# Plain v loaded in pieces of six block columns, with a newly searched fixed order, in a kernel of windowed attention and a gated convolution

## The chip, the core and the metric

The kernel runs on one core of a Trainium2 chip. Five engines work side by side, each through its own queue of instructions in program order: PE (matrix multiply; its weight loads are shown as PEld), DVE (vector), ACT (scalar, exponentials and copies), POOL (general purpose) and SP, which in this kernel only issues DMAs. All DMAs of the kernel are issued from SP, and 16 DMA engines carry them out. The metric is the device time of one execution in microseconds. Three executions of the kernel before took 174.15, 173.76 and 173.53 us; the median is 173.76.

## The reference

Eight batches of eight heads, 576 tokens, 64 features per head. Heads 0 to 3 ("plain") look back over the last 32 tokens, heads 4 to 7 ("dilated") over every fourth of the last 128. The attention's output, 512 features per token, then goes through a gated block: a causal convolution of length 5 gives the gate, a projection gives the value, and a second projection gives the result.

```python
scores = scale * np.matmul(q, k.transpose(0, 1, 3, 2))
mask_plain = (rel >= 0) & (rel < window)
mask_dil = (rel >= 0) & (rel < window * dilation) & (rel % dilation == 0)
attn = softmax(where(mask, scores, -1e9))
x = np.matmul(attn, v)                     # heads side by side: 8 x 576 x 512
gate_pre += conv_w[k][None, None, :] * xp[:, k:k + S, :]     # k = 0..4
gate = 1.0 / (1.0 + np.exp(-gate_pre))
return (gate * (x @ w_val) @ w_out).astype(np.float32)
```

## The kernel before

The program is a list of 733 small tasks, each tied to one engine and to named buffers. A task's name says what it is and of which batch (0 to 7):

- loads on SP: `Lqd`, `Lkd`, `Lvd` bring q, k, v of the dilated heads of a batch, `Lqp`, `Lkp`, `Lvp` those of the plain heads, `Lwv` and `Lwo` the two projection weights, `Lc` the convolution's. For batches 0 and 7 the last fifth of a dilated q or k is a load of its own (`Lqr`, `Lkr`). `ST` stores 128 finished tokens.
- `T` transposes q or k on PE, five matmuls for a dilated half and eighteen for a plain tensor (lines 464 and 401). `E` with q or k in its name copies the result out of PSUM on ACT or DVE (lines 312, 314).
- `S` makes scores of one half (six matmuls, line 333), `E` the exponential on ACT (line 340), `M` the mask multiply on DVE (line 347), `A` the product with v (twelve matmuls, line 356), `N` the division by the row sums on DVE (lines 365, 366). `X` transposes the result back on PE (lines 428, 488), `F` copies it into the gated block's input.
- `U` casts dilated v to bf16 on POOL. For batches 0 to 3 plain v is loaded in natural rows of tokens, and the four shift tasks `HA`, `HB`, `HC`, `HD` (2, 3, 3 and 2 small casts on POOL or ACT, table `SHIFTS`) build the windows that straddle the blocks. For batches 4 to 7 the windows overlap already in the load, and no shift is needed.
- for each pair of batches and each block of tokens, `C` is the convolution on PE (twenty matmuls, line 530), `G` the tanh on ACT, `V` the value projection (eight matmuls, line 548), `Y` the gating on DVE (line 558). `O` is the output projection of 128 tokens (four matmuls, line 577), `EO` its copy out of PSUM (ACT line 584, DVE line 586).
- `Wv` and `Wo` cast the projection weights on POOL; no `V` can start before the three `Wv` tasks, no `O` before the two `Wo`.

The order of everything is fixed by hand-written data. `ORDER` is one word per task: its number, a letter for the engine that runs it, and a number of warm-up matmuls (128x128 by 128x512, line 659) that PE does in front of it into the same PSUM buffer; `HOMES` gives each logical tile its buffer, from `COUNTS` (eight for q and k, two for plain v, three two-bank PSUM tiles, two one-bank ones). Each engine works its words off from left to right, and an engine waits at the head of its queue until the data and the buffer are there. Loads have one rule more: a load waits until the fifth-last "big" load before it has landed (`DEPTH = 5`, `t.after`). The semaphores add another: DMAs take eight semaphores in turn, and a DMA waits for the landing of the one eight places before it in SP's queue.

Before the change plain v of a batch was one DMA, `load_vp`: 18 block columns of 128 rows (2304 packets of 256 bytes) for batches 0 to 3, 24 of them (3072 packets) for batches 4 to 7, counted as a big load.

Of the kernel before, what the change touches and what calls it, by code (L numbers as in the profile page):

```python
# [16 lines left out]
0G 15S 16S 1S 13S 33P6 14S 34A 48S 17S 47S 49S 2P 31P1 32A 3V 18G 38P2 57P 51G 21P 59V 22V 53G 58V 52G 39A 40V  # L17
19P 35P 20A 26P2 36A 23P 80S 27A 37V 24A 28V 25V 41P2 54P 56A 4S 55A 42V 29P 30V 70P 81S 6G 45P3 5G 43P 50A
60P 73P 7S 46V 71A 44A 74A 8G 112S 61A 96P 84P 63P 64A 149P 72V 97A 75V 76P 98P 85V 65V 62V 82S 66P 77V 86P
67V 150A 99A 100P 78P 87A 101A 83G 103P 88P 89A 79V 68P 69V 104A 113S 105V 119P 114S 120A 91P 92A 145P 151P  # L20
93V 102V 90V 121A 94P 169S 146A 152V 106P 95V 147P 122P 107V 108P 170S 110P 123V 124A 138P 109A 201S 139A 148V
135P 185P 136A 125P 128P 129A 126A 111V 165P 166A 140V 130V 137V 116G 127V 186V 234S 202S 157P 158A 187P 115G
118G 117G 141P 171S 175P 176A 188V 192P 193A 131P 142V 132V 173P 172G 174A 189P 190A 208P 209V 210A 143P 133P
177P 178A 180P 203S 134V 211P 235S 250P 144V 159P 181A 213A 212A 227P 228A 153P 154A 11S 238P 205G 251V 194V
179V 191V 160V 182V 239A 206A 195P 229V 196V 207A 167P 168V 204G 12G 183P 184V 155P 252P 224P 225A 214P 240P
215A 9S 253V 156V 199P 254P 241V 255A 226V 217P 218A 161P 230P 197P 162A 200A 324S 267S 236S 216V 219V 245P
256V 220P 198A 246A 231V 10G 625P 628P 221V 323S 266S 325S 237G 626A 257P 242P 243A 276P 629A 222P 326G 223A
258A 278A 277V 163P 341P 232P 303P 247V 244V 259V 233V 342V 304A 299P 300A 164V 339P 260P 248P 329P 305P 330A
340V 268S 261V 631P 630S 355S 384S 533S 627S 346P 356S 249V 343P 264P 306V 265V 273P 632A 347A 344A 348V 274V
275A 272A 345V 262P 301P 302V 279P 280A 292P 634P 635V 263A 349P 350V 327P 293A 328A 289P 281V 282P 283A 290A  # L30
# [72 lines left out]
class Plan:  # L103
# [28 lines left out]
    def run(self):  # L132
# [4 lines left out]
        for word in order:  # L137
# [19 lines left out]
def kernel(  # L157
# [19 lines left out]
    QB = 96  # L177
# [49 lines left out]
    def src_ap(t, offset, ap):  # L227
        return bass.AP(tensor=t.tensor, offset=t.offset + offset, ap=ap)
# [480 lines left out]
```

## Time and profile before

| | us |
|---|---|
| median of three executions | 173.76 |
| the profiled execution, its own time | 173.37 |
| its span, first to last instruction | 171.7 |
| PE busy | 153.0 |
| DVE busy | 121.7 |
| ACT busy | 108.4 |
| POOL busy | 44.2 |

The span is what the trace shows; the time of the execution has 1.7 us more around it. Times of instructions are counted from the span's start. "PE busy" counts pipelined matmuls with modelled ends, so that small idle stretches can hide in it. In the views "A:B" is a stretch of the span, "[1.01 <-DMA ...]" the idle time of an engine in front of an instruction and what ended it, and rows marked "SPq" are DMAs as SP issues them: their duration is the time that the issue held SP, not that of the transfer.

### The profile page before, as it was taken

Reading aid. Unit: us, or ns where it says so; the run is one execution under the profiler, and the core shown is the slowest. Engines: PE = TensorE matmul, PEld = TensorE weight load, DVE = VectorE, ACT = ScalarE, POOL = GpSimd, SP = SyncE. Lnnn points to the kernel's source line nnn. Section 1 sums busy time; section 2 is a strip of 40 time slices with the busy share of each in tenths; the row PEclk is TensorE's granted clock in tenths of the full one; section 3 lists DMA queues with packets and bytes.
Section 4 is the critical chain, followed back from the end, with each engine's and each line's share of the span. In section 5 each row is a group of like instructions: output and inputs, shape, how many; then the busy total and the mean of one; then the engine's idle time right before and its main releaser. Section 6 shows DMA issues by size and latency. Waiting matters only on the chain.

```text
span 171.7 us, 5752 instructions
## 1 busy us (share of the span) xinstructions
PE 153.0 (89%) x2441; PEld 102.2 (60%) x2460; DVE 121.7 (71%) x243; ACT 108.4 (63%) x182; POOL 44.2 (26%) x82
## 2 busy tenths in 40 slices
PE   6697967888989979899999799989999999999990
PEld 1355654677557546567766567576656577666640
DVE  6549778989899579779788658899368776664220
ACT  2147976198868744798847693888946675242542
POOL 7023998560659427403000000210110000000000
PEclk9999999999999999999999999999999999999999
DMA  4999999999799999999994948969979060333445
GB/s 137 325 355 290 375 370 210 311 374 319 200 383 364 362 269 281 373 353 222 282 328 139 267 115 286 373 165 390 270 202 303 2 244 4 116 119 138 186 165 199
DMA packets 49123, 43.63 MB, mean 254 GB/s; under 512 B 22981, under 2 KB 39365, under 8 KB 49098
## 3 DMA queue, kind: packets, MB, share of 16 engines
q1 hardware_dynamic: 49098, 43.27, 82.2%
q8 instruction: 19, 0.31, 0.7%
q14 instruction: 6, 0.05, 0.1%
HBM read 33.83 MB, written 9.44 MB: 252 GB/s over the span
## 4 chain that ended last, share of the span: by engine, by line
PE 58%; DMA 12%; DVE 11%; ACT 6%; SPq 5%; issue 3%; POOL 3%; ACTq 0%; DVEq 0%; POOLq 0%
PE pu L577 17%; PE pd L548 14%; PE pd L530 9%; DMA qk<-in_k_dram 5%; PE pd L356 5%; DVE et L347 4%; DMA wt<-in_moe_w_out_dram 4%; SPq L281 4%; PE pd L333 4%; DMA qk<-in_q_dram 3%; PE pu L464 3%; POOL w_out L316 3%; PE pd L401 2%; PE pu L488 2%; ACT et L340 2%
## 5 line engine op out<-in xcount | busy, mean ns | idle before, releaser
L340 ACT ACTIVATE et<-pd 128x576 bf16<-128x576 f32 x64 | 39.3, 657 | 10.4 <-PE pd L333 9.3
L347 DVE TENSOR_TENSOR et<-et,mask 128x576 bf16<-128x576 bf16 x64 | 33.9, 557 | 4.7 <-ACT et L340 4.5
L548 PE MATMUL pd<-xT,w_val 128*128 128x384 bf16 (+1 forms) x208 | 34.9, 313 | 0.7 <-DVE xn L366 0.4
L577 PE MATMUL pu<-w_out,yT 128*128 128x512 bf16 x127 | 33.4, 379 | 1.4 <-issue 0.6
L558 DVE SCALAR_TENSOR_TENSOR yT<-gate,pd 128x768 bf16<-128x768 bf16 (+1 forms) x26 | 23.0, 886 | 12.5 <-PE pd L548 8.5
L366 DVE TENSOR_TENSOR xn<-pd,rec 96x768 bf16<-96x768 f32 x32 | 30.5, 954 | 1.1
L316 POOL CAST vn<-vd 128x1536 bf16<-128x1536 f32 x8 | 12.3, 1540 | 70.3 <-DMA vd<-in_v_dram 70.3
L540 ACT ACTIVATE gate<-pd 128x768 bf16<-128x768 f32 (+1 forms) x26 | 19.9, 769 | 10.9 <-DVE yT L558 5.5
L548 PEld LDWEIGHTS <-w_val 128*128 128x128 bf16 x208 | 19.4, 97 | 11.6 <-issue 1.5
L530 PE MATMUL pd<-xT,conv_diag 64*64 64x384 bf16 (+1 forms) x520 | 23.1, 313 | 1.8 <-DVE xT L314 1.1
L584 ACT ACTIVATE osb<-pu 128x512 f32<-128x512 f32 x27 | 16.2, 601 | 11.0 <-PE pu L577 10.7
L577 PEld LDWEIGHTS <-yT 128*128 128x128 bf16 x144 | 12.6, 97 | 13.3 <-issue 1.1
L333 PE MATMUL pd<-qT,kT 64*128 64x96 bf16 x384 | 16.1, 209 | 3.1 <-ACT qT L312 0.9
L530 PEld LDWEIGHTS <-conv_diag 64*64 64x64 bf16 x520 | 15.1, 106 | 6.2 <-issue 2.5
L316 POOL CAST vw<-vp 32x384 bf16<-32x384 f32 (+2 forms) x31 | 16.8, 541 | 7.5 <-DMA vp<-in_v_dram 6.1
L356 PEld LDWEIGHTS <-et 128*128 128x128 bf16 x384 | 14.7, 97 | 6.5 <-DVE et L347 2.5
L464 PE MATMUL pu<-ident,qk 128*128 128x128 bf16 x160 | 14.8, 230 | 3.0 <-DMA qk<-in_k_dram 2.0
L333 PEld LDWEIGHTS <-kT 64*128 64x128 bf16 x384 | 10.1, 96 | 11.5 <-issue 6.3
L464 PEld LDWEIGHTS <-qk 128*128 128x128 bf16 x160 | 10.8, 102 | 7.3 <-DMA qk<-in_k_dram 3.0
L314 DVE COPY xT<-pu 128x576 bf16<-128x576 bf16 x18 | 10.1, 568 | 4.0 <-PE pu L488 3.1
L312 ACT COPY xT<-pu 128x576 bf16<-128x576 bf16 x14 | 8.9, 646 | 6.2 <-PE pu L428 3.6
L365 DVE RECIPROCAL rec<-pd 96x12 f32<-96x12 f32 x32 | 7.1, 223 | 7.6 <-PE pd L356 4.5
(52 smaller groups left out, 146.2 us busy)
## 6 DMA issues: line engine op xcount, KB each, us to landing
out_dram<-osb SPq DMA_DIRECT2D x36, 256.0 KB, 2.7
vd<-in_v_dram SPq DMA_DIRECT2D x8, 768.0 KB, 9.3
qk<-in_k_dram SPq DMA_DIRECT2D x8, 576.0 KB, 7.8
qk<-in_q_dram SPq DMA_DIRECT2D x8, 576.0 KB, 8.0
qk<-in_q_dram SPq DMA_DIRECT2D x6, 640.0 KB, 9.1
qk<-in_k_dram SPq DMA_DIRECT2D x6, 640.0 KB, 8.7
vp<-in_v_dram SPq DMA_DIRECT2D x4, 768.0 KB, 7.9
vp<-in_v_dram SPq DMA_DIRECT2D x4, 576.0 KB, 9.8
```

What stands on the lines that cost most here:

```text
L316: nc.gpsimd.tensor_copy(out_, in_)
L333: nc.tensor.matmul(out=ps2[ps.idx][:, l, QB * jj:QB * jj + QB], lhsT=kT[kt.idx][rb, c:c + 128], rhs=qT[qt.idx][rb, c:c + QB], start=True, ...
L340: nc.scalar.activation(out=et[e.idx][:, 0:2 * HW].rearrange("p (l n) -> p l n", l=2), in_=ps2[ps.idx][:, :, 0:HW], func=AF.Exp, scale=scale)
L347: (nc.vector if eng == DVE else nc.gpsimd).tensor_tensor(out=ev, in0=ev, in1=m, op=ALU.mult)
L356: nc.tensor.matmul(out=ps2[po.idx][:, hf, (2 * jj + l) * DA:(2 * jj + l + 1) * DA], lhsT=et[es[hf].idx][:, c:c + 128], rhs=val(j, l), star ...
L366: nc.vector.tensor_tensor(out=xn[xt.idx][0:QB].rearrange("p (h j) l d -> p h (j l) d", h=2), in0=a[:, :, :, 0:D], in1=rr[:, :, :, None].to ...
L464: nc.tensor.transpose(out=o[:, f:f + 128], in_=a[:, c * RD + 128 * cb:c * RD + 128 * cb + 128], identity=ident)
L530: nc.tensor.matmul(out=dst(ps2[pc.idx][64 * ob:64 * ob + 64, n, 0:wd]), lhsT=conv_diag[rb, 2 * cp + n, kk, :], rhs=mov(2 * cp + n, rb, c0 ...
L540: nc.scalar.activation(out=gate[gt.idx][:, :, 0:wd], in_=ps2[pc.idx][:, :, 0:wd], func=AF.Tanh, scale=0.5)
L548: nc.tensor.matmul(out=dst(ps2[pv.idx][:, n, 0:wd]), lhsT=w_val[:, mc, c * 128:(c + 1) * 128], rhs=mov(mc, slice(0, 128), c0), start=(mc = ...
L558: nc.vector.scalar_tensor_tensor(out=yT[yb.idx][:, 2 * cp:2 * cp + 2, t0:t0 + wd], in0=gate[gt.idx][:, :, 0:wd], scalar=1.0, in1=ps2[pv.id ...
L577: nc.tensor.matmul(out=ps1[po.idx], lhsT=yT[yb.idx][:, c, c0:c0 + 128], rhs=w_out[:, c, :], start=(c == 0), stop=(c == NCH - 1))
```

## The change

`load_vp` now makes three DMAs (batches 0 to 3) or four (4 to 7), each of six block columns, 768 packets. They don't count as big, so that they wait for a big load but no later load counts them. The four numbers of `SHIFTS` that are durations for the search's model are changed; the program doesn't read them. `ORDER` and `HOMES` are new throughout: 753 words, 20 of them the added loads.

```diff
-0G 15S 16S 1S 13S 33P6 14S 34A 48S 17S 47S 49S 2P 31P1 32A 3V 18G 38P2 57P 51G 21P 59V 22V 53G 58V 52G 39A 40V
...
+0G 15S 1S 16S 33P6 2P 13S 14S 34V 48S 31P1 32A 59P2 51S 38P 35P 36A 39A 47S 50S 17S 21P 3V 18G 19P 20A 61A 22A
...
-            if t.load:
+            if t.load and eng == SP:
                 t.after = big[-DEPTH] if len(big) >= DEPTH else None
...
     def load_vp(b, ten):
         nat = b < NAT
 
-        def issue():
-            if nat:
-                o, a = vp[ten.idx][:, 0:18, 0:D], [[D, 128], [128 * D, 18], [1, D]]
-            else:
-                o, a = vp[ten.idx][:, :, 0:D], [[D, 128], [QB * D, 4 * NB], [1, D]]
-            return nc.sync.dma_start(out=o, in_=src_ap(v, (b * H * S - (0 if nat else W)) * D, a))
-        return [load(f"Lvp{b}", ten, issue)]
+        def issue(c):
+            o = vp[ten.idx][:, c:c + 6, 0:D]
+            step = 128 if nat else QB
+            return nc.sync.dma_start(out=o, in_=src_ap(v, (b * H * S - (0 if nat else W) + c * step) * D,
+                                                       [[D, 128], [step * D, 6], [1, D]]))
+        parts = [lambda c=c: issue(c) for c in range(0, 18 if nat else 4 * NB, 6)]
+        return [load(f"Lvp{b}", ten, part, big=False) for part in parts]
```

The engines' shares of the tasks change too. DVE has 185 tasks where it had 173: it takes three more output copies `EO` (12 for 9), 3 more dilated k copies, 1 plain k, 2 dilated q, 3 plain q; of the copies into the gated block's input it takes 2 more dilated and 2 fewer plain ones. ACT has 166 for 176: it loses those, and gains one `HA` and one `HC` from POOL (24 for 26). PE does the same 265 tasks; the warm-up matmuls in front of them are 23 for 16.

SP's queue, in the stretch from plain k of batch 0 on. Names ending in a number are buffers: `qk2` holds plain k of batch 0, `vd0` and `vp0` dilated and plain v of batch 0. Before:

```order
L270 DMA qk2_70<-in_k_dram 128x2x576
L290 DMA vd0_80<-in_v_dram 128x6x256
L270 DMA qk3_71<-in_q_dram 128x2x576
L302 DMA vp0_76<-in_v_dram 128x18x64
L281 DMA qk4_72<-in_q_dram 128x5x256
L627 DMA wt0_82<-in_moe_w_val_dram 128x2x512
L281 DMA qk5_73<-in_k_dram 128x5x256
L627 DMA wt1_83<-in_moe_w_val_dram 128x2x512
L270 DMA qk6_74<-in_q_dram 128x2x576
L290 DMA vd1_81<-in_v_dram 128x6x256
```

The same stretch after the change, from the same load on:

```order
L271 DMA qk2_70<-in_k_dram 128x2x576
L301 DMA vp0_76<-in_v_dram 128x6x64
L271 DMA qk3_71<-in_q_dram 128x2x576
L301 DMA vp0_76<-in_v_dram 128x6x64
L291 DMA vd0_80<-in_v_dram 128x6x256
L301 DMA vp0_76<-in_v_dram 128x6x64
L282 DMA qk4_72<-in_k_dram 128x5x256
L282 DMA qk5_73<-in_q_dram 128x5x256
L282 DMA qk6_74<-in_k_dram 128x5x256
L271 DMA qk7_75<-in_k_dram 128x2x576
L291 DMA vd1_81<-in_v_dram 128x6x256
L628 DMA wt0_82<-in_moe_w_val_dram 128x2x512
```

Dilated v of batch 0 moves behind plain q and two of the three pieces of plain v. Dilated k and q of batch 1 now come before the value weights, and dilated k of batch 2 (`qk6`) stands between them and plain k of batch 1. Plain q of batch 1 (`qk6` before), fifth behind `vp0`, comes only after this excerpt.

POOL's queue around the casts of the output weights (`w_out`, tasks `Wo`) and of plain v of batch 2 (`vp0` into `vw0`, tasks `H`). Before:

```order
L316 CAST vn0_85<-vd0_80 128x24x64
L316 CAST vw0_78<-vp0_76 32x5x64
L316 CAST vw0_78<-vp0_76 32x6x64 x2
L316 CAST vw0_78<-vp0_76 64x6x64 x2
L316 CAST w_out_129<-wt2_84 128x512
L316 CAST w_out_129<-wt2_84 64x512 x2
L316 CAST w_out_129<-wt0_82 64x512 x4
```

And after:

```order
L317 CAST w_out_129<-wt2_84 128x512
L317 CAST w_out_129<-wt2_84 64x512 x2
L317 CAST vn0_85<-vd0_80 128x24x64
L317 CAST vw0_78<-vp0_76 64x6x64 x2
L317 CAST vw0_78<-vp0_76 32x5x64
L317 CAST vw0_78<-vp0_76 32x6x64 x2
L317 CAST w_out_129<-wt0_82 64x512 x4
```

Three of the seven weight casts move ahead of the casts of batch 2; the other four now follow those of plain v directly.

More of the change, by code (lines that the diff above doesn't have):

```diff
@@ L22 @@
[L22 to L30, printed above, removed]
-284V 271G 270G 269G 643P 644A 637P 285P 291V 294V 400P 401V 286V 638A 334P 331P 335A 332A 336V 640P 641A 295P
```

59 lines of the change are left out of this document (35 added, 24 removed), and 6 rows, old and new, of the table SHIFTS.

## Prediction

> **What bounds the kernel now.** I read the page first, then sums by stretch, then PE's idle times, then SP's queue.
>
> ```profile
> PE 153.0 (89%) x2441; PEld 102.2 (60%) x2460; DVE 121.7 (71%) x243; ACT 108.4 (63%) x182; POOL 44.2 (26%) x82
> PE 58%; DMA 12%; DVE 11%; ACT 6%; SPq 5%; issue 3%; POOL 3%; ACTq 0%; DVEq 0%; POOLq 0%
> 0.00:36.00 36.00, 28.00 (x435) 18.07 (x438) 26.61 (x75) 19.54 (x33) 21.41 (x54) 1.00 0.97 301
> 56.30:168.10 111.80, 106.52 (x1654) 70.90 (x1670) 76.82 (x136) 71.73 (x123) 11.76 (x14) 1.00 0.76 229
> ```
>
> The columns of the last two rows are the stretch, its length, PE, PEld, DVE, ACT, POOL busy, granted clock, DMA share, GB/s. Over the whole span PE is the bound, but not everywhere: up to 36 us it is idle for 8 us while the DMAs are busy 97% of the time, and from 56.3 us to its last matmul it is idle for 5.28 us of 111.8. So the first stage is fed by loads, the rest is PE's own work with small holes. The clock is full throughout and is no term here.
>
> ```profile
> 22.46 0.45 PE L464 MATMUL pu<-ident,qk 128*128 128x128 bf16 x5 [1.01 <-DMA qk<-in_k_dram]
> 30.01 0.92 PE L356 MATMUL pd<-vn,et 128*128 128x65 bf16 x24 [1.04 <-DVE et L347]
> 63.50 1.00 PE L530 MATMUL pd<-xT,conv_diag 64*64 64x384 bf16 x18 [1.12 <-DVE xT L314]
> ```
>
> These are PE's longest holes behind a load, a mask and a copy. The change aims at the first kind. Why a load is late there, SP's queue shows:
>
> ```profile
> 4.97 0.78 SPq L302 DMA_DIRECT2D vp<-in_v_dram  x1
> 7.82 5.54 SPq L281 DMA_DIRECT2D qk<-in_q_dram  x1
> 22.43 0.37 SPq L302 DMA_DIRECT2D vp<-in_v_dram  x1
> 23.82 5.13 SPq L281 DMA_DIRECT2D qk<-in_q_dram  x1
> 38.26 5.67 SPq L281 DMA_DIRECT2D qk<-in_k_dram  x1
> ```
>
> In these three cases (the third plain v was issued just ahead of the last row) the DMA behind a plain v holds SP for 5 us, where others take 0.4 to 1: 2304 packets do not fit at once, and SP stands until they have nearly drained. What that costs the DMA engines is in the rows around the second and third such load:
>
> ```profile
> 27.00:28.00 1.00, 0.92 (x16) 0.44 (x8) 0.52 (x3) 1.00 (x3) 1.00 (x4) 1.00 1.31 245
> 28.00:29.00 1.00, 0.97 (x6) 0.39 (x4) 1.00 (x1) 0.71 (x1) 1.00 (x1) 1.00 1.09 193
> 29.00:30.00 1.00, 0.00 (x0) 0.00 (x0) 1.00 (x3) 0.00 (x0) 0.28 (x1) 1.00 0.26 56
> 30.00:31.00 1.00, 0.99 (x25) 0.92 (x26) 0.96 (x3) 0.00 (x0) 0.00 (x0) 1.00 0.66 138
> 31.00:32.00 1.00, 1.00 (x7) 0.58 (x6) 1.00 (x2) 0.00 (x0) 0.40 (x1) 1.00 1.02 339
> 42.00:43.00 1.00, 0.39 (x16) 0.42 (x16) 0.62 (x2) 1.00 (x2) 0.00 (x0) 1.00 1.31 234
> 44.00:45.00 1.00, 1.00 (x11) 0.46 (x10) 1.00 (x3) 0.73 (x2) 0.72 (x1) 1.00 0.25 62
> ```
>
> The small packets run at 245 GB/s, larger ones at 339 and more, but between them there is a hole at 56 and 62 GB/s.
>
> **The change part by part.** I follow two gates, then the rest.
>
> **(a) The holes.** Against the rates beside it the first hole shown loses (245-193)/245 + (245-56)/245 + (339-138)/339 = 0.21 + 0.77 + 0.59 = 1.6 us of transfer. The one at 44 us has the same depth, so 1.6 again. Two holes are 3.2 us by the time the first 24 large loads are in. A piece of 768 packets is as many as a dilated v, whose successors were issued without such a stand. I take the whole 3.2; the bounds are 0 (pieces leave holes too) and 3.2.
>
> **(b) The output weights' gate.** The first output projection needs all seven weight casts.
>
> ```profile
> 50.82 5.49 POOL L316 CAST w_out<-wt 128x512 bf16<-128x512 f32 x7 [1.68 <-DMA wt<-in_moe_w_out_dram]
> 55.89 2.14 PE L577 MATMUL pu<-w_out,yT 128*128 128x512 bf16 x7
> L316 POOL CAST vw<-vp 32x384 bf16<-32x384 f32 x21 | 11.5, 547 | 2.0 <-DMA vp<-in_v_dram 1.0
> L316 POOL CAST w_out<-wt 64x512 bf16<-64x512 f32 x6 | 4.6, 764 | 0.3
> ```
>
> Now the casts end at 50.82 + 5.49 = 56.3 us, just when PE gets there. The last of the 24 loads (through the second half of `w_out`) landed about 52.2: the first half at 50.7, where the casts begin, and 0.52 MB more at 339 GB/s, 1.5 us. After the change the same 24 loads are in front, only the last is the third piece of plain v of batch 2. Without holes it lands at 52.2 - 3.2 = 49.0. POOL then does `HA`, `HB` (5 x 0.547 = 2.7) and four weight casts (4 x 0.764 = 3.1): the gate moves to 54.8. With the holes kept it would be 58.0.
>
> **(c) Does PE get there by then?** PE's own prices come from runs of its tasks without a wait:
>
> ```profile
> 101.16 0.36 PE pd L333 x12
> 101.89 1.30 PE pd L548 x8
> 103.19 0.86 PE pu L577 x4
> 106.66 0.28 PE pu L464 x5
> 106.94 0.94 PE pd L530 x20
> 113.19 0.39 PE pd L356 x12
> 114.18 0.46 PE pu L488 x16
> ```
>
> A plain transpose of q or k takes 0.62, eighteen matmuls at nearly the price of L464's. Up to the transpose of plain k of batch 2 (ending at 43.2 us before) and up to the last dilated score of batch 2 in the new order, both orders have done exactly the same PE tasks, so these two times may be compared. The late load in the new order is plain q of batch 1, now behind dilated k of batch 2. The loads of dilated q of batch 2 and of plain q of batch 1 before, with the time from issue to landing last:
>
> ```profile
> qk<-in_q_dram SPq DMA_DIRECT2D x1, 640.0 KB, 9.5
> qk<-in_q_dram SPq DMA_DIRECT2D x1, 576.0 KB, 9.4
> ```
>
> Issued at 23.82, the first landed at 33.3. The new set up to plain q of batch 1 lacks that load, half of the value weights and two thirds of a plain v, and has one more dilated k of the same size: 0.52 MB (1.5 us at 339 GB/s) and 1536 small packets (1.6 us at 245) less, so 30.2, or 28.6 without the hole at 29 us. I take 29.5. Before, issued at 15.87, it came at 25.3: PE's use of it moves 4 us back, but some 1.5 us of other tasks now stand in front of it. From its transpose (to 30.1) to the common point lie 12.3 us of PE work by the prices above, warm-ups included: 42.4 if nothing waits. Waits I expect: scores of batch 1 behind two ACT copies, 0.5; the first `V` behind the last `Wv` cast, 0.3; the product of batch 1 behind `HC`, `HA` on ACT, 0.5. So **43.7 against 43.2** before, bounds 42.4 and 45.5: no gain in the first stage itself, since the queue brings the same bytes and the new order spends its lead on the wrong load. The seven extra warm-ups are in these sums, 7 x 0.215 = 1.5 us, most in front of tasks that wait for a load anyway; where that cover is gone they cost up to that.
>
> From the common point to the first `O` the new order has 10.8 us: PE arrives at 54.5, and the gate of (b) is at 54.8. Against 56.3 that is **-1.5 us**, bounds -1.5 (the gate holds it even if PE is early) and +1.7 (holes kept). At that point it has one `V` (1.30) more and one `X`, half an `A` and an `S` (0.46 + 0.39 + 0.18) less behind it: **-0.3**.
>
> **(d) The rest, 56 to 168 us.** PE's tasks are the same. No load is near: by the same count of bytes the closest, dilated k of batch 4, lands near 61 and is used near 64. Behind it SP's queue stands at the second store until that output is copied, near 61 too; dilated v of batch 4 and the q loads of 4 and 5 wait behind it, and PE wants them from 72 on. The eight semaphores now cover five large loads and three pieces at a time, some 3.7 MB or 10 us of transfer, so that this wait starves nothing. DVE gets more copies:
>
> ```profile
> L586 DVE TENSOR_SCALAR osb<-pu 128x512 f32<-128x512 f32 x9 | 6.2, 685 | 2.2 <-PE pu L577 2.2
> L314 DVE COPY kT<-pu 128x576 bf16<-128x576 bf16 x6 | 2.7, 446 | 0.0
> L314 DVE COPY kT<-pd 128x576 bf16<-128x576 bf16 x6 | 4.5, 754 | 5.6 <-PE pu L428 3.1 <-PE pd L401 2.2 <-ACT kT L312 0.3
> 30.00:40.00 10.00, 8.98 (x196) 7.03 (x197) 9.29 (x17) 5.90 (x10) 5.38 (x10) 1.00 1.03 345
> 50.00:60.00 10.00, 9.84 (x172) 6.42 (x173) 7.61 (x14) 7.10 (x14) 6.66 (x8) 1.00 1.08 364
> 110.00:120.00 10.00, 9.45 (x211) 6.99 (x211) 9.53 (x18) 8.92 (x17) 1.68 (x1) 1.00 0.89 293
> ```
>
> Three output copies (2.1), five dilated q and k (2.2), four plain (3.0) and the exchanged `F` copies (up to 0.6) are some 7.5 us. A DVE busy 76% left PE 0.16 us idle in ten, one at 93 to 95% left it 0.55 and 1.02. About half the copies fall between 60 and 100 us; if all four stretches of ten there went from the first figure to the last, that would be 4 x 0.86 = 3.4 us. Bounds 0 and 3.4; I take **+0.7**, nearer to nothing because DVE is busy 76.82 of 111.8 us there, 69%. ACT and POOL lose work, and their waits may shrink; I count nothing for it.
>
> **(e) The end.** Before, two output projections stand between the last `V` and the first that needs its gating, now one (0.86 us). `Y` there takes about 0.75 and has two handovers: **+0.15**, bounds 0 and 0.3.
>
> **Sum.** The profiled execution took 173.37, 0.39 less than the median. 173.37 - 1.5 - 0.3 + 0.7 + 0.15 = 172.4; on the median's footing **172.8**.
>
> **The rivals.**
>
> *PE's holes after 56 us close too.* The order was redrawn there as well, and the new one puts more PE work between a task and its user in the first stage. If half of the 5.28 us closes and DVE costs nothing: 172.8 - 2.6 - 0.7 = 169.5. Against it: nothing in the change feeds that stage better, and 95% is already high.
>
> *DVE becomes the late engine.* At the 3.4 us bound, and with the gate's gain kept, 172.8 + 2.7 = 175.5. It decides once DVE passes some 93% over several stretches of ten. For it: DVE holds the longest hole of the rest (1.12, a copy). Against: of the stretches of ten after 60 us only the one at 110 is there now.
>
> *The first stage slips.* Plain q of batch 1 and dilated v of batch 0 come later by 4 and 3 us; if the holes stay and PE reaches the common point at 45.5, the lead is lost and PE gets to the first `O` at 58.0, the gate's other bound: 172.8 + 3.2 = 176.0. Against it: SP's stands of 5 us are plain, and shorter loads behind other loads had none.
>
> *It doesn't do what it says.* The holes close but were hidden: PE reaches the first `O` at 56.3 as before, and what it has done ahead by then (0.3) goes to DVE: 173.8. For it: (c) gives the first stage itself no gain, and PE's way to the gate of (b) has 0.3 us to spare.
>
> *Each DMA has its own price.* Twenty more issues at 0.37 to 1.0 us of SP are 7 to 20 us of an engine that waits most of the time; if a third of the smaller sum came in front of loads that PE needs, 2.5 us: 175.3. Against it, two loads issued one behind the other, 0.5 us apart:
>
> ```profile
> qk<-in_k_dram SPq DMA_DIRECT2D x1, 512.0 KB, 4.2
> qk<-in_k_dram SPq DMA_DIRECT2D x1, 128.0 KB, 4.0
> ```
>
> They land 0.3 us apart, as the smaller one's bytes take. The Trainium skill, DMA: Bandwidth & Descriptors, Rules for kernel authors, speaks against this change: many small transfers should be coalesced into one large one. Its fixed cost of about 2.0 us for each DMA (Anatomy of one DMA, there told of another issuing path) would, paid in a row, make an estimated 40 us for the twenty; by the two rows above it is not paid in a row here.
>
> **How the numbers follow.** A measurement here can tell about 0.3% from no change, 0.5 us. Chances: the forecast 0.38, the holes after 56 us 0.12, DVE 0.20, the slip 0.12, no effect 0.13, SP's price 0.05. The forecast's own range is 171.0 to 174.3, so it holds 0.30 of faster, 0.05 of same, 0.03 of slower. With the others: faster 0.30 + 0.12 + a little of no effect (0.02) = 0.44; same 0.05 + 0.11 = 0.16; slower 0.03 + 0.20 + 0.12 + 0.05 = 0.40. The range 170.0 to 176.0 leaves out half of the second case and the worst of DVE and the slip.
>
> **What would show it.** (a) No issue on SP over 2 us behind plain v before 50 us, and no stretch of 1 us near 60 GB/s. (b) The last weight cast ends near 54.8. (c) PE's last transposes of batch 2 end near 43.7. (d) PE idle from the first `O` to its end 5 to 7 us. Wrong: PE waiting for loads after 60 us, DVE above 93% in several stretches, or the first `O` after 56.3.

## The result and the profile after

Twelve executions of the changed kernel took 173.45 to 174.86 us, median 173.89; twelve of the kernel before 173.22 to 175.22, median 173.86. The ratio is 1.0001, interval 0.9977 to 1.0026: no difference that can be measured, where 172.8 was forecast. (Ratios, here and below, leave out executions that were disturbed, so that one need not be the quotient of two medians.) The profiled execution took 173.49 (before 173.37), its span is 171.7 in both.

The equal times hide two changes of opposite sign. The first two fences are after's page (busy times, chain of waits) and its table by stretches, with the columns of the prediction's.

```profile
PE 154.4 (90%) x2445; PEld 103.0 (60%) x2467; DVE 127.7 (74%) x255; ACT 105.4 (61%) x175; POOL 42.2 (25%) x77
PE 65%; DMA 13%; DVE 10%; SPq 4%; ACT 3%; issue 2%; ACTq 0%; DVEq 0%
```

```profile
28.00:29.00 1.00, 1.00 (x23) 0.65 (x15) 1.00 (x3) 0.59 (x2) 1.00 (x2) 1.00 1.15 288
29.00:30.00 1.00, 0.45 (x11) 0.24 (x7) 1.00 (x4) 1.00 (x2) 1.00 (x3) 1.00 1.10 323
44.00:45.00 1.00, 0.59 (x19) 0.54 (x17) 0.91 (x3) 0.97 (x2) 0.00 (x0) 1.00 1.16 326
58.63:168.30 109.67, 106.56 (x1685) 71.19 (x1700) 82.71 (x147) 67.90 (x114) 10.94 (x12) 1.00 0.70 223
```

DVE is busy 6 us more (127.7), and the chain runs over PE for 65% of the span, not 58, over ACT and POOL for 3, not 9. The holes in the transfer are gone: 323 GB/s at 29 us where before had 56, 326 at 44 us where it had 62. And yet PE's way through the first stage is longer. PE's queue in order of time, at the three places that count:

```profile
30.96 0.69 PE L402 MATMUL pd<-ident,qk 128*64 128x128 bf16 x18 [1.50 <-DMA qk<-in_q_dram]
45.35 0.30 PE L334 MATMUL pd<-qT,kT 64*128 64x96 bf16 x6
58.25 0.24 PE L357 MATMUL pd<-vw,et 128*128 128x65 bf16 x2 [1.26 <-DVE et L348]
58.63 1.02 PE L578 MATMUL pu<-w_out,yT 128*128 128x512 bf16 x3
```

Plain q of batch 1 is waited for until 30.96; the common point, the end of the row at 45.35, is at 45.65 (before 43.24); the first `O` starts at 58.63 (before 55.89). From there to its end PE idles 109.67 - 106.56 = 3.11 us, where it idled 5.28 from 56.30 on before. So 2.7 us are lost up to the first `O` and some 2.5 won behind it.

What holds the first `O`, on POOL and then on DVE:

```profile
50.23 3.24 POOL L317 CAST vw<-vp 64x384 bf16<-64x384 f32 x5 [7.63 <-PE pu L465]
53.53 2.71 POOL L317 CAST w_out<-wt 64x512 bf16<-64x512 f32 x4
56.31 1.58 POOL L317 CAST vn<-vd 128x1536 bf16<-128x1536 f32 x1
```

```profile
55.19 3.00 DVE L348 TENSOR_TENSOR et<-et,mask 128x576 bf16<-128x576 bf16 x3
```

The weights' last cast ends at 56.24, no earlier than before (56.31). The three masks of plain batch 2 run beside POOL's casts and take 3.00 us (the last of them 1.71), where the same three take 1.19 in a run below. SP's longest stand up to 50 us is this one, right behind a piece of plain v; five more issues right behind a piece stand 2.02 to 2.60 us:

```profile
5.89 2.67 SPq L291 DMA_DIRECT2D vd<-in_v_dram  x1
```

### The profile page after: what moved, and what is told of

The parts are those of the page before. It is cut to its first block, busy times and chain, and to the rows that moved or that the text cites. A ratio compares the mean times of both kernels' runs of the same rounds, so it can differ in the third digit from the quotient of the medians.

```text
span 171.7 us, 5799 instructions
## 1 busy us (share of the span) xinstructions
PE 154.4 (90%) x2445; PEld 103.0 (60%) x2467; DVE 127.7 (74%) x255; ACT 105.4 (61%) x175; POOL 42.2 (25%) x77
## 4 chain that ended last, share of the span: by engine, by line
PE 65%; DMA 13%; DVE 10%; SPq 4%; ACT 3%; issue 2%; ACTq 0%; DVEq 0%
PE pu L578 17%; PE pd L549 17%; DMA qk<-in_q_dram 10%; PE pd L531 10%; PE pd L357 5%; PE pd L334 5%; DVE xn L367 3%; PE pu L465 3%; PE pd L402 3%; PE pu L489 2%; DMA qk<-in_k_dram 2%; PE pu L429 2%; DVE et L348 2%; SPq L291 2%; SPq L301 2%
## 5 line engine op out<-in xcount | busy, mean ns | idle before, releaser
L348 DVE TENSOR_TENSOR et<-et,mask 128x576 bf16<-128x576 bf16 x64 | 32.2, 534 | 6.6 <-ACT et L341 6.6
L531 PE MATMUL pd<-xT,conv_diag 64*64 64x384 bf16 (+1 forms) x520 | 23.7, 314 | 0.2
L585 ACT ACTIVATE osb<-pu 128x512 f32<-128x512 f32 x24 | 14.3, 599 | 10.7 <-PE pu L578 10.0
L357 PEld LDWEIGHTS <-et 128*128 128x128 bf16 x384 | 15.3, 97 | 8.0 <-DVE et L348 2.1
L334 PE MATMUL pd<-qT,kT 64*128 64x96 bf16 x384 | 16.7, 207 | 3.3 <-ACT kT L313 0.6
L317 POOL CAST vw<-vp 32x384 bf16<-32x384 f32 (+2 forms) x26 | 16.0, 615 | 12.9 <-PE pu L465 7.6
L531 PEld LDWEIGHTS <-conv_diag 64*64 64x64 bf16 x520 | 14.2, 106 | 4.6 <-issue 0.7
L465 PEld LDWEIGHTS <-qk 128*128 128x128 bf16 x160 | 10.2, 102 | 6.3 <-DMA qk<-in_q_dram 2.4
L402 PE MATMUL pd<-ident,qk 128*64 128x128 bf16 x288 | 11.1, 228 | 2.8 <-DMA qk<-in_q_dram 1.5
L402 PEld LDWEIGHTS <-qk 128*64 128x64 bf16 x288 | 9.4, 115 | 5.3 <-DMA qk<-in_k_dram 1.6
```

Source lines behind the costliest of these rows:

```text
L317: nc.gpsimd.tensor_copy(out_, in_)
L334: nc.tensor.matmul(out=ps2[ps.idx][:, l, QB * jj:QB * jj + QB], lhsT=kT[kt.idx][rb, c:c + 128], rhs=qT[qt.idx][rb, c:c + QB], start=True, ...
L348: (nc.vector if eng == DVE else nc.gpsimd).tensor_tensor(out=ev, in0=ev, in1=m, op=ALU.mult)
L357: nc.tensor.matmul(out=ps2[po.idx][:, hf, (2 * jj + l) * DA:(2 * jj + l + 1) * DA], lhsT=et[es[hf].idx][:, c:c + 128], rhs=val(j, l), star ...
L402: nc.tensor.transpose(out=o[64 * y:64 * y + 64, 128 * j:128 * j + 128], in_=a[:, (y * PJ + j) * D:(y * PJ + j + 1) * D], identity=ident)
L465: nc.tensor.transpose(out=o[:, f:f + 128], in_=a[:, c * RD + 128 * cb:c * RD + 128 * cb + 128], identity=ident)
```

## The experiments

Ratios are to the kernel before, run beside each on the same chip.

### The holes, the pieces and the order, each alone

*Order of before, plain v in pieces, one issued right behind the other:*

```diff
 def load_vp(b, ten):
...
+            for c in range(0, 18 if nat else 4 * NB, 6):
+                got.append(nc.sync.dma_start(
+                    out=vp[ten.idx][:, c:c + 6, 0:D],
...
```

> The order before, with each plain v issued as three or four DMAs of 768 packets one behind the other. If the size of a DMA alone makes the holes in the transfers, they close here too: no stretch of 1 us near 60 GB/s at 29 and 44 us, the loads behind land 1.5 us earlier each time, and by the rigid theory the time falls by up to 1 us, by the absorbed one it stays within 0.5. If it needs other loads between the pieces, SP is still held 4 to 5 us by the third piece or the load behind it, the holes stay, and the time is that of before, 173.8.

Measured: 173.58, ratio 0.9994 (0.9962 to 1.0026). First SP's queue, then the stretches at the second plain v:

```profile
22.39 4.56 SPq L300 DMA_DIRECT2D vp<-in_v_dram  x3
27.06 2.07 SPq L281 DMA_DIRECT2D qk<-in_q_dram  x1
```

```profile
29.00:30.00 1.00, 0.00 (x0) 0.00 (x0) 1.00 (x3) 0.00 (x0) 0.39 (x1) 1.00 1.05 133
30.00:31.00 1.00, 0.88 (x25) 0.85 (x26) 1.00 (x3) 0.00 (x0) 0.00 (x0) 1.00 0.48 121
```

SP stands no shorter than before, only now mostly at the pieces themselves (4.56 + 2.07, before 0.37 + 5.13), and a hole of 133 and 121 GB/s stays. So it is the 2304 small packets in a row that hold SP, not that they were one DMA. Together with the next run, where the new order without pieces holds SP again, this says that other loads between the pieces are what closes the hole.

*Order of after, plain v whole at the place of its last piece:*

```diff
         def issue(c):
+            n = 18 if nat else 4 * NB
+            if c + 6 < n:
+                return None
...
```

> The changed kernel with plain v whole again: one DMA at the place of the last piece, nothing at the others. The holes of 1.5 us come back in the first 60 us. Rigid: PE's first output projection 1 to 3 us later than at 58.6, time 175 to 177. Absorbed: within 0.5 of 173.9. If the pieces were of no use in this order, PE's arrival there does not move either.

Measured: 175.65, ratio 1.0115 (1.0069 to 1.0161). SP's queue, then PE's:

```profile
21.69 6.52 SPq L271 DMA_DIRECT2D qk<-in_q_dram  x1
```

```profile
32.33 0.69 PE L404 MATMUL pd<-ident,qk 128*64 128x128 bf16 x18 [1.77 <-DMA qk<-in_q_dram]
```

SP stands 6.52 us at plain q of batch 1, and PE has it 1.4 us later than in after. In the new order the pieces are worth about 2 us (1.2 to 2.8 by the interval); in the old one (the run above) nothing that can be measured.

### The late load of plain q

*After, with plain q of batch 1 loaded ahead of dilated v of batch 1, and transposed ahead of that batch's first product with v:*

```diff
-... 65P 55A 73A 75P 174S 89A 115S 84S ... 4S 5G 43P 69V 44V 6G 118S 114S 116S ... 96P 123P ...
+... 65P 55A 73A 75P 174S 89A 115S 114S 84S ... 4S 5G 43P 69V 44V 6G 118S 116S ... 123P 96P ...
```

> The changed kernel with plain q of batch 1 loaded ahead of dilated v of batch 1, and its transpose ahead of the first dilated product of batch 1. Two theories. Rigid: PE's order is the chain to the end, so what PE loses in the first stage costs as much at the end; the load should land near 27 instead of 30.9, PE should reach the first output projection 1.0 to 1.5 us earlier than at 58.6, and the time should fall by the same to 172.3 to 172.9. Absorbed: PE's lateness in the first stage is found again in the rest, where copies and casts run ahead while PE is late; PE reaches the first output projection earlier, but the time stays at 173.6 to 174.1. A third way: the weight casts behind dilated v of batch 1 come 1.6 us later and take the place of the wait, and neither moves.

Measured: 174.35, ratio 1.0034 (1.0004 to 1.0064); first `O` at 59.61. PE's queue:

```profile
30.30 0.69 PE L402 MATMUL pd<-ident,qk 128*64 128x128 bf16 x18 [1.44 <-ACT gate L541]
32.79 0.59 PE L660 MATMUL pd<-warm 128*128 128x512 bf16 x1 [0.93 <-DVE xn L367]
```

The wait stays and only changes its name: with the load there, PE waits 1.44 behind a `G` on ACT, and then 0.93 behind an `N` on DVE. The load is one of several things that end together near 30 us. In this execution the granted clock was 0.85 from 30 to 34 us and 0.82 from 34 to 40, where after's was 1.00, which may be part of why its first `O` is 1 us later than after's.

What PE had done by then shows the loss more plainly than any wait. The rows are the stretches to 31 us and from there to the common point, first of before, then of after; the last rows of each are the same stretches for the warm-up line alone (PE, PEld, clock, DMA share, GB/s).

```profile
0.00:31.00 31.00, 23.88 (x349) 15.11 (x352) 21.92 (x69) 17.33 (x28) 17.42 (x46) 1.00 0.96 290
31.00:43.24 12.24, 10.56 (x238) 8.31 (x237) 10.91 (x19) 8.58 (x15) 5.38 (x10) 1.00 1.11 347
...
0.00:31.00 31.00, 6.23 (x14) 1.57 (x16) 1.00 0.96 290
```

```profile
0.00:31.00 31.00, 22.72 (x318) 14.24 (x322) 22.24 (x70) 16.07 (x26) 13.31 (x29) 1.00 0.98 300
31.00:45.65 14.65, 13.67 (x276) 9.99 (x278) 11.01 (x21) 11.30 (x20) 10.80 (x27) 1.00 1.09 342
...
0.00:31.00 31.00, 7.34 (x18) 2.00 (x20) 1.00 0.98 300
31.00:45.65 14.65, 0.76 (x2) 0.23 (x3) 1.00 1.09 342
```

Without warm-ups before has done 23.88 - 6.23 = 17.65 us of work at 31 us, after 22.72 - 7.34 = 15.38: 2.3 us behind, which is the common point's 2.4. PE's waits put down to a load sum to 4.2 us in after up to there and to 2.8 in before, its other waits to about 4 in both; the 1.1 us of warm-ups that after has more (7.34 against 6.23) mostly fill further waits, as the section on them shows. After had moved more bytes by then (300 against 290 GB/s), but dilated k of batch 2 and a piece of plain v of batch 1 had come ahead of the second half of the value weights, which landed at 33.1 (in before at 23.8); before had cast those weights and did its first `V` at 27.51, after does its first at 36.82. That the loads' order caused the 2.3 us is read from these figures; the next run was to test it.

*After, with dilated k of batch 2 and the second half of the value weights swapped, and their work with them* (7 and 8 are the weights' load and cast, 155 the first `V`; 174 is the load of dilated k, 191 and 179 are its transposes):

```diff
-... 75P 174S 89A ... 102P 191P 103A ... 179P 180A ... 7S 8G 96P 123P ... 120G 155P 151P ...
+... 75P 7S 89A ... 8G 85G ... 174S 155P 96P 123P ... 191P 133A ... 179P ... 180A ... 120G 151P ...
```

> The order of after with the load of dilated k of batch 2 and that of the second half of the values' weights swapped (about as long, 1.5 to 1.9 us), and their work with them: the first w_val product goes from 36.8 us to ahead of the first dilated product of batch 1 with v (28.8), the transposes of dilated k of batch 2 go behind the first convolution (36). Theory L, which work the loads allow by 31 us makes the common point late: the 1.46 us of w_val fill the hole of 1.50 us ahead of plain q of batch 1, useful work at 31 us rises by 0.7 (1.46 less the two transposes of 0.37) or more, common point 0.7 to 1.5 us earlier than 45.6; the first O follows only as far as the mask of 1.71 us (1.26 of wait) and the last weight cast at 56.2 let it, time 172.6 to 173.6, ratio 0.993 to 0.999. Rival N, the hole stays because the w_val product waits for its cast or its x, or plain q lands later: common point within 0.4 of 45.6, time 173.6 to 174.4.

Measured: 179.73, ratio 1.0343 (1.0312 to 1.0375). PE's queue, then POOL's:

```profile
32.03 0.50 PE L549 MATMUL pd<-xT,w_val 128*128 128x384 bf16 x1 [3.38 <-POOL w_val L317]
```

```profile
26.59 1.47 POOL L317 CAST vn<-vd 128x1536 bf16<-128x1536 f32 x1 [1.58 <-DMA vd<-in_v_dram]
28.02 5.03 POOL L317 CAST w_val<-wt 64x128 bf16<-64x128 f32 x16
```

The hole grew, and behind it the granted clock was 0.70 from 30 to 34 us and 0.63 from 34 to 40. I had overlooked that the first half's sixteen casts stand behind `U` of batch 1 on POOL and take 5.03 us, and that a `V` needs both halves. The run doesn't tell whether earlier weights help; it shows that loading them earlier is of no use while their casts come late. So the cause of the 2.3 us stays argued, not shown. The same edit with the cast of the next section moved as well:

> The run before and GpSimd's cast of dilated v of batch 3 behind the last mask of plain batch 2. If the two terms add: first O near 56.3, held there by the last cast of the output weights, time 171.0 to 172.0, ratio 0.985 to 0.991. If the casts at 56.2 or the masks of plain batch 2 gate it anyway: 172.0 to 172.8, as with the cast alone.

Measured: 179.54, ratio 1.0276 (1.0222 to 1.0330), with the same wait of 2.99 us; it adds nothing.

### The warm-ups

*After with 16 warm-ups, as before, not 23:*

```diff
-... 26P5 ... 90P1 ... 78P1 ... 139P2 ...
+... 26P2 ... 90P ... 78P ... 139P ...
```

> The order of after with 16 warm-up matmuls as in before, not 23: three of the five ahead of the first dilated score of batch 0, the one ahead of a dilated score of batch 1, the one ahead of plain batch 0's product with v, and both ahead of a plain score of batch 1 are left out (they compute nothing that is used). Up to the common point PE is busy 1.9 us longer in after than in before, 1.3 of it with warm-ups by the time they take alone. Theory W, they stand on TensorE's path: common point 0.8 to 1.9 us earlier than 45.6 (43.7 to 44.8), first O as much earlier, time 172.0 to 173.1, ratio 0.990 to 0.996. Rival F, they fill waits that are there anyway: common point within 0.3 of 45.6, time 173.6 to 174.0, ratio 0.998 to 1.002. Second rival, the clock falls without them: granted clock under 0.98 and time 1 us or more longer.

Measured: 175.23, ratio 1.0100 (1.0064 to 1.0137), granted clock 0.967 to 1.0 over its six executions (after: 0.99 to 1.0 over twelve). A row of its stretches and a row of its PE queue, and then the same two of after, in four fences:

```profile
34.00:40.00 6.00, 6.00 (x85) 3.86 (x82) 2.16 (x4) 3.86 (x7) 5.41 (x14) 0.55 1.07 364
```

```profile
35.49 3.41 PE L531 MATMUL pd<-xT,conv_diag 64*64 64x384 bf16 x40
```

```profile
34.00:40.00 6.00, 5.98 (x102) 3.99 (x101) 4.26 (x8) 5.78 (x11) 5.47 (x14) 1.00 1.07 372
```

```profile
34.67 1.93 PE L531 MATMUL pd<-xT,conv_diag 64*64 64x384 bf16 x40
```

Behind the wait for plain q (1.49 us here) the granted clock falls to 0.55, and forty matmuls take 3.41 us, not 1.93. That is the second rival of the expectation as far as the time goes; whether the warm-ups are the reason, the next run puts in doubt. It is the same edit together with the cast of the next section, and its profiled execution had a clock of 0.997:

> The order of after with both edits: 16 warm-ups (seven left out, which compute nothing that is used) and the cast of dilated v of batch 3 behind the last mask of plain batch 2. If the warm-ups stand on the path and the mask's second does too, their gains add: 0.8 to 1.9 and 0.9, time 171.1 to 172.2, ratio 0.985 to 0.991. If the first O's gate is the casts of the output weights at 56.2 by then, only the mask's part is left: 172.5 to 173.0, ratio 0.993 to 0.996.

```profile
45.64 1.46 PE L552 MATMUL pd<-xT,w_val 128*128 128x384 bf16 x8 [0.17 <-ACT et L341]
```

The `V` behind the common point starts at 45.64, in after at 45.81: where the clock holds, the seven warm-ups cost 0.17 us or nothing, since they fill waits. (Single traces don't resolve 0.17: a run below with the order of before up to there, e7, passes the common point 0.55 earlier than before.) Over its twelve executions this kernel ran from 172.47 (clock 0.999) to 176.43 (0.961), ratio 0.9999 (0.9962 to 1.0036). In six of the twelve the clock was 0.98 or lower. In the next run, which differs from this one only in having all 23 warm-ups, it was so in five of twelve. The first run against after (0.99 or higher in all twelve) speaks for warm-ups that keep the clock up, this pair against it; it isn't shown. Nor is the clock the whole of the first run's loss: two of its executions at 0.998 and 1.0 took 175.07 and 174.58. The first run's trace has a hole of 0.88 us ahead of a convolution at 118 us, which after lacks; the rest stays open.

### The mask beside the cast

*After, with GpSimd's cast of dilated v of batch 3 (`U`) waiting for the last mask of plain batch 2:*

```diff
         def cast(eng):
-            copy(eng, vn[tn.idx][:, :, :, 0:D], vd[tv.idx].rearrange("p j (c d) -> p j c d", c=R))
+            r = nc.gpsimd.tensor_copy(vn[tn.idx][:, :, :, 0:D], vd[tv.idx].rearrange("p j (c d) -> p j c d", c=R))
+            if b == 3:
+                tc.add_manual_dep(r.ins, masks["p2"][-1].ins.name, ...
```

> The order of after with one more wait: GpSimd's cast of dilated v of batch 3 (1.58 us from 56.31) starts only after the last mask of plain batch 2, beside which it ran (that mask took 1.71 us, others of its form 0.45). Theory M, the mask beside a GpSimd cast is what holds the first O: the mask takes 0.45 to 0.6, the first O comes 1.1 us earlier, near 57.5, and with the rest at 109.5 the time is about 172.8, ratio 0.994. Rival, another gate stands right behind (the output weights' last cast at 56.2, ScalarE's copies of plain v of batch 2): the mask gets short, and the first O moves by less than 0.5, time 173.5 to 173.9. Second rival, the cast is now late for batch 3 and TensorE waits for it: up to 1 us longer than after.

Measured: 172.46, ratio 0.9952 (0.9920 to 0.9984). Its DVE, POOL and PE queues:

```profile
56.89 1.19 DVE L348 TENSOR_TENSOR et<-et,mask 128x576 bf16<-128x576 bf16 x3
```

```profile
58.29 1.47 POOL L449 CAST vn<-vd 128x1536 bf16<-128x1536 f32 x1 [2.27 <-DVE et L348]
```

```profile
47.07 1.46 PE L552 MATMUL pd<-xT,w_val 128*128 128x384 bf16 x8 [0.17 <-ACT et L341]
...
58.89 1.03 PE L581 MATMUL pu<-w_out,yT 128*128 128x512 bf16 x3
```

The masks take 1.19, not 3.00, PE's wait of 1.26 is gone, and from the `V` behind the common point to the first `O` it is 58.89 - 47.07 = 11.82 us, in after 58.63 - 45.81 = 12.82. The profiled execution reached the common point 1.3 us later, at a granted clock of 0.89 up to there, so that the weights' casts, too, were over before the masks began. The run with fewer warm-ups and the same wait has no such delay, and there the first two masks still run beside those casts:

```profile
55.02 1.73 DVE L348 TENSOR_TENSOR et<-et,mask 128x576 bf16<-128x576 bf16 x3
```

Its first `O` is at 57.19, 11.55 us behind the `V` at 45.64, 1.27 less than in after. So 1.0 to 1.3 us of the first stage's loss is this collision, and nobody waits for the later cast.

### Does the late start shorten the rest?

*Before, with ten warm-ups ahead of the transpose of plain q of batch 1:*

```diff
-... 113S 105V 119P 114S 120A ...
+... 113S 105V 119P10 114S 120A ...
```

> The kernel before with ten warm-up matmuls more in front of the transpose of plain q of batch 1: PE is held 2.15 us longer at 25 us, nothing else changes. Rigid: 173.86 + 2.1 = 176.0. Absorbed: the holes after 56 us (5.3 us in sum) shrink by what is added, time 173.8 to 174.5.

Measured: 173.97, ratio 1.0030 (1.0001 to 1.0058). The 2.15 us of work disappear in the waits of the first stage: the first `O` comes at 55.76, as before, and so the run says little on the rest.

The orders can be joined, since at the common point and at the first `O` both have done nearly the same. The bar marks the seam in `ORDER`; behind it come the words of the other order that are not yet there, and `HOMES` is adapted.

```diff
+e5: ... 208S 209S 138V 217P 241S | 11S 218V 219A 9S 185A ...   (before, then after, at the common point)
+e6: ... 138V 242S 276S 148V 273S | 176G 256P 163P 233P 234A ... (after, then before, at the common point)
+e7: ... 202A 252A 237V 10G 645P | 276S 272S 248P 275S 249A ... (before, then after, at the first O)
```

> The order of before (plain v in its pieces, one behind the other, where before had it whole) up to the common point, which the profile of before passes at 43.2 us and that of after at 45.6; from there the order of after. Theory A, the stages are rigid and add up: the first O comes near 56 or earlier, the stretch from it to TensorE's end is 109.5 as in after, the span some 169.3 and the time about 171.3, ratio about 0.986 to before. Theory B, the short rest of after is paid for by the later start (loads, casts and vector work run ahead while TensorE is late): an earlier first O only lengthens the rest to 111-112, time 173 to 174, ratio 0.995 to 1.003. Something between, an O near 58 because the waits of 45 to 58 us belong to the order of after and not to its later start, and a rest of 109.5: 173.3 to 173.9, and then the stage between the common point and O is what costs, not the one before it.

> The mirror of the run before: the order of after with its spread pieces up to the common point, then the order of before. Theory A (stages add up): the common point near 45.6, the first O near 58.3, the rest 111.9, time about 176, ratio 1.013. Theory B (a late start is won back by whatever follows): common point near 45.6, rest 109.5 to 110.5, time 173.5 to 174.3, ratio 0.998 to 1.003.

> As the first of these, but the order of before is kept up to the first output matmul, so that the stage between the common point and O is the one of before too. Theory A: first O near 56.0, rest 109.5, span about 169.5, time about 171.5, ratio 0.987. Theory B: first O near 56.0, rest 111.5 to 112.3, time 173.5 to 174.3. If this run gains and the other does not, the loss of the new order lies between the common point and O.

Measured, in this order: 173.99, ratio 1.0015 (0.9978 to 1.0053); 176.46, ratio 1.0200 (1.0156 to 1.0243); 172.05, ratio **0.9917 (0.9883 to 0.9950)**. The rest of the third (stretches, then PE's queue), and of the second (stretches):

```profile
54.58:166.20 111.62, 107.30 (x1660) 70.73 (x1674) 83.55 (x147) 67.84 (x114) 11.46 (x14) 1.00 0.73 232
```

```profile
114.19 1.01 PE L531 MATMUL pd<-xT,conv_diag 64*64 64x384 bf16 x20 [0.95 <-DVE xT L315]
```

```profile
57.78:172.90 115.12, 108.47 (x1661) 72.35 (x1674) 78.26 (x138) 72.01 (x122) 12.03 (x14) 0.99 0.68 212
```

The worse half of each together (e6) is the slowest of the three, the better half of each (e7) the fastest, and it beats before by 0.8%, where after ties. In e6 the rest of before follows a first `O` at 57.78 and is not shorter for it: PE idles 115.12 - 108.47 = 6.65 us in it. (The profiled execution took 178.15; four of the six took 176.3 to 176.5, still far from theory B's 173.5 to 174.3.) e7 by its parts fits neither theory: both had the first `O` near 56.0, and it came at 54.58; the rest, 111.4 to PE's last matmul, lies by theory B's 111.5 to 112.3, not at A's 109.5. But of what it has more than after, 0.95 is one hole in front of a convolution, which five other runs with the order of after in the rest have too (0.61 to 0.94), while after has no such row, and 0.7 is PE work left over at the seam (107.30 busy, in after 106.56). The hole's cause stays open. What decides against B is the ten traces with the order of after and its engines behind the common point: with the first `O` anywhere from 57.19 to 65.10, the rest to PE's last matmul is 109.5 to 110.7 us, and 109.5 in after and 110.0 at 65.10. A later start doesn't shorten it.

The gain of e7 isn't shown to come from the shorter rest. Its profiled execution, the fastest of its six (171.33), has the first `O` 1.31 us earlier than before, with the same order up to there, and only some 0.5 us won behind it. Pieces alone (the first run above) don't bring that: its first `O` is at 56.02. Why e7 is early there stays open.

e5 lost its gain at the seam. With the cast of the section above moved too:

> The order of before to the common point, the order of after from there, and GpSimd's cast of dilated v of batch 3 behind the last mask of plain batch 2. Theory A (stages add up, and the mask beside the cast is one term): against the same mixture without the wait, whose third mask took 1.71 us and whose TensorE waited 1.25 us for it, the first O comes 1.0 to 1.2 us earlier; time 171.5 to 172.9, ratio 0.989 to 0.996. Rival: the wait of 1.6 us at the seam (43.3 to 45.6 in the mixture without the wait) and the lower clock behind it decide, and the mask only takes its slack: time 173.5 to 174.3, ratio 0.999 to 1.004.

Measured: 173.84, ratio 1.0029 (1.0005 to 1.0052). PE's queue:

```profile
44.85 1.46 PE L552 MATMUL pd<-xT,w_val 128*128 128x384 bf16 x8 [1.59 <-ACT kT L313]
```

The first part ends at 43.3, as in before, and there PE stands 1.59 us behind a copy of k on ACT, which neither order alone has at that place. The rival of that expectation was right.

### The copies' engines

43 copies out of PSUM behind the first `O` run on another engine in after than in before. *Before, with the engines of after there, and the mirror, after with the engines of before* (letters of words changed, some 6 us to or from DVE):

```diff
-e11 (before): ... 223A ... 278A ... 233V ... 342V ... 330A ...
+              ... 223V ... 278V ... 233A ... 342A ... 330V ...
-e15 (after):  ... 239A ... 286V ... 229V ... 282A ... 350A ...
+              ... 239V ... 286A ... 229A ... 282V ... 350V ...
```

> The order of before, plain v whole, in which from the first O on the copies out of PSUM run on the engine that after gives them (43 change between ScalarE and VectorE, in sum some 6 us more on VectorE). Theory C, the copies' engines make the rest short in after: the holes behind ScalarE (0.58, 0.88 us) and VectorE (1.12, 0.32, 0.50) between 60 and 115 us shrink, idle time after the first O 2.6 to 3.6 instead of 4.7, time 171.5 to 172.7, ratio 0.989 to 0.995. Rival P, it is the order on TensorE that hides them: idle time 4.4 or more, and 6 us more on VectorE cost the 0.7 of the forecast or more: 173.6 to 176, ratio 1.000 to 1.014.

> The order of after, in which from the first O on 43 copies out of PSUM run on the engine that before gives them (some 6 us less on VectorE, 4 more on ScalarE). Theory P2, engines and order are fitted to each other, whichever they are: idle time after the first O rises from 2.7 to 5 or more, time 176 to 180, as in the mirror case, which had 8.9 of idle time. Rival C2, fewer copies on VectorE are simply better: idle time 2.7 or less, time 173.0 to 173.9. Rival C3, ScalarE becomes late, since it has the exponentials and the gates: idle time 3 to 4, 174 to 175.5.

Measured: 179.84, ratio 1.0355 (1.0316 to 1.0394), and 179.04, ratio 1.0301 (1.0274 to 1.0329). The rest of the first and one of its PE rows, then the rest of the second and one of its:

```profile
55.60:174.50 118.90, 109.42 (x1661) 71.85 (x1674) 83.30 (x146) 67.36 (x113) 12.06 (x14) 0.99 0.71 216
```

```profile
135.28 0.53 PE L488 MATMUL pu<-ident,xn 96*64 96x96 bf16 x16 [1.42 <-DVE osb L586]
```

```profile
58.58:173.90 115.32, 107.22 (x1685) 71.28 (x1700) 77.02 (x138) 72.04 (x123) 10.41 (x12) 1.00 0.67 211
```

```profile
163.72 1.02 PE L578 MATMUL pu<-w_out,yT 128*128 128x512 bf16 x4 [1.17 <-ACT osb L585]
```

DVE and ACT are as busy in the first as in after (83.30 and 67.36 us, in after 82.71 and 67.90); in after PE idles 3.11 us, here 9.48. The mirror, with before's light DVE (77.02), idles 8.10. So neither set of engines is better: each fits the order it was made with, and either half of the pair alone costs 5 to 6 us.

## Why the prediction was wrong

- **(a) The holes: right in kind, too large.** No stretch is near 60 GB/s, and stands of 5 us are gone; but the sign named, no issue over 2 us behind plain v, did not come: six stand 2.02 to 2.67. Of the 3.2 us of transfer, after is 0.87 MB ahead at 46 us (314 against 295 GB/s up to there), 2.6 us at the 339 GB/s of the prediction, and only 0.5 MB or 1.5 us at 50 (312 against 302), since its own rate sinks to 253 and 250 GB/s from 47 to 49. The runs add why the holes close: packets of other loads in between, not shorter DMAs.
- **(b) The gate: mis-sized.** The casts ended at 56.24, not 54.8. The third piece of plain v landed at 50.1 (forecast 49.0), POOL's five shift casts began at 50.23 and took 3.24 (2.7); the weights' four took 2.71 (3.1). It wasn't the gate that counted: the masks on DVE ended 2 us later.
- **(c) The step that failed.** Plain q was awaited until 30.96 (forecast 29.5), and the common point came at 45.65 (43.7, bounds 42.4 and 45.5): 1.5 of these 1.95 us are the late load. I had followed this one load and the work behind it. Loading it earlier doesn't bring the time back, so that it wasn't the bound alone; after is 2.3 us of work behind at 31 us, and that the other loads of the new order cause this is argued, not shown. From the common point to the first `O` the forecast had 11.1 us without a wait for DVE; it took 12.98, of which 1.26 are the wait for the masks beside POOL's cast, and PE was busy 11.46 of them, where 10.8 was forecast. The first `O` came at 58.63, forecast 54.8. Against before's 55.89 it is 2.74 later, where 1.5 earlier was forecast (the forecast counted from 56.3, the end of before's last weight cast). The rival that the first stage slips gave 45.5 and 58.0, right in place, but by holes that stay; they did not.
- **(d) Wrong in sign.** Some 7.5 us of copies more on DVE were to cost 0.7, and ACT's relief was to bring nothing; PE was to idle 5 to 7 us. From the first `O` to its end PE idles 3.11 us and needs 2.5 us less. That the same engines for the copies cost 6 us in the old order shows that the step's method, a price for each copy by DVE's share, doesn't work here. Of the holes of before, rows 63.50 of the prediction and these,

```profile
73.38 0.54 PE L356 MATMUL pd<-vn,et 128*128 128x65 bf16 x12 [0.58 <-ACT et L340]
97.45 0.43 PE L333 MATMUL pd<-qT,kT 64*128 64x96 bf16 x12 [0.88 <-ACT qT L312]
112.77 0.41 PE L428 MATMUL pu<-ident,xn 96*128 96x96 bf16 x6 [0.50 <-DVE qT L314]
```

  none is left in after, which has two of its own:

```profile
92.80 0.30 PE L334 MATMUL pd<-qT,kT 64*128 64x96 bf16 x6 [0.64 <-ACT kT L313]
93.52 0.30 PE L334 MATMUL pd<-qT,kT 64*128 64x96 bf16 x6 [0.41 <-ACT gate L541]
```

  That PE's holes after 56 us close was a rival at 0.12; it came true at nearly the size given there (2.2 us of 2.6).
- **The warm-ups:** taken as 1.5 us in (c)'s sum, most of it under waits. On PE's way they cost no more than 0.17 where the clock holds.
- **The sum.** Counted against before, the first `O` was 4.2 us off in the one direction (2.74 + 1.5), the rest 3.1 in the other (2.54 less, where 0.3 less and 0.85 more were forecast); 173.49 against the 172.4 forecast for the profiled execution is what was left of it. That the time came near the forecast is luck: two errors of 3 to 4 us cancel. Two rivals each gave one half of the truth, and none had them together.

## What to carry to other kernels

Where loads bound a stage, ask of a new order of loads how much useful work they allow by a given time, not only when the one late load lands: here 10 GB/s more up to 31 us went with 2.3 us less work done. An order and its choice of engines are one thing: price them together or by a run, since half of a fitted pair costs more (5 to 6 us here) than either whole gains. Where two versions tie, cut both at points that they share and join the halves: that gave the fastest kernel here (0.9917 of before), though its trace doesn't show the gain where the join was to bring it, and the join at the common point gave nothing (e5, without and with the moved cast). One wait that separates a GpSimd cast from masks on the path gave 0.9952.

## What the runs showed of the hardware

- A mask multiply on DVE, both of whose inputs lie in SBUF, stands while a POOL cast runs: three of them take 3.00 us beside casts, 1.19 beside none; one alone took 1.71 beside a cast of 1.58, where 0.4 is its share of the 1.19. The Trainium skill, SBUF — State Buffer, Who interferes with whom, has this as an exclusive lock, taken for a whole instruction, between such a DVE instruction and a GpSimd one that reads SBUF; the rows agree.
- PE's granted clock fell to 0.55 for 6 us behind a stretch in which PE was busy 3.25 us of 4 and 2.83 of 4, with no wait over 1.5 us; in after it stayed at 1.00 behind 3.26 and 2.78 and a wait of 1.50. First the run with fewer warm-ups, then after:

```profile
26.00:30.00 4.00, 3.25 (x60) 2.12 (x56) 4.00 (x9) 3.07 (x6) 2.76 (x4) 1.00 1.10 315
30.00:34.00 4.00, 2.83 (x60) 2.40 (x60) 2.58 (x5) 2.63 (x6) 3.79 (x16) 0.82 1.10 334
```

```profile
26.00:30.00 4.00, 3.26 (x60) 2.28 (x60) 4.00 (x9) 2.83 (x5) 2.80 (x4) 1.00 1.13 317
30.00:34.00 4.00, 2.78 (x67) 2.07 (x70) 2.60 (x5) 3.09 (x7) 3.79 (x16) 1.00 1.01 310
```

  So PE's busy time by these stretches doesn't tell when the clock falls. The Trainium skill, TensorE: Matmul & The Clock Gate, HAM oscillation — how this bites in real kernels, gives as its rule that no idle gap be longer than about 3.4 us; here the clock fell with gaps less than half as long. Variants with all 23 warm-ups showed it too (0.85 from 30 to 34 us and 0.82 from 34 to 40 in the run with plain q first), and whether warm-ups make it rarer stays open (a clock of 0.98 or lower in six of twelve executions without seven of them, in five of twelve with all, both with the cast behind the masks).
- 2304 packets of 256 bytes held SP 4.6 to 6.9 us, whether as one DMA (at the next issue: 5.54, 5.13 and 5.67 in before) or as three in a row (at themselves: 4.56 in the row shown, 6.87 at most).
